# Sorted block attention with a token-mixing MLP: w_out among the casting loads, loads that wait for a batch's V, and a new order

## The chip, the core and the metric

The kernel runs on one core of a Trainium2 chip. The metric is the device time of one execution in microseconds; several executions are timed and the median is given. One execution was taken with the hardware profiler; times "at 33.27" are microseconds from the start of its span. A core has TensorE (PE: matmuls and transposes into PSUM, with its weight loads PEld), VectorE (DVE), ScalarE (ACT), GpSimd (POOL) and SyncE (SP). DMAs are issued by SP or POOL and carried out by 16 DMA engines. A load that changes the type on the way (float32 in memory, bfloat16 in SBUF) is issued by POOL.

## The reference

Four batches, 8 heads, 768 positions of 64, cut into 8 blocks of 96. A matrix P per head (8x8, from `sort_net` by five rounds of softmax-like normalisation) mixes the blocks of K and of V; attention runs inside each block; the result is put through a token-mixing MLP.

```python
P = sort_net
for _ in range(5):
    P = P - np.max(P, axis=-1, keepdims=True)
    P = np.exp(P)
    P = P / (np.sum(P, axis=-1, keepdims=True) + 1e-09)
    P = P / (np.sum(P, axis=-2, keepdims=True) + 1e-09)
k_sorted = einsum('bhij,bhjcd->bhicd', P, k_b);  v_sorted likewise
attn = softmax(q_b @ k_sorted_b.T / 8);  x = attn @ v_sorted_b        # per block
wq, wk = x @ w_q, x @ w_k
W_tok = einsum('bsd,btd->bst', wq, wk) / 8
out = relu(einsum('bst,btd->bsd', W_tok, x)) @ w_out
```

## The kernel before

All work is cut into small items, each one call of a function `u_<letter>`. The string `ORDER` (L18 and on) lists them in the order in which they are issued, and since every engine runs its instructions in that order, the string is the schedule. An item is a letter, a batch, a number and a last sign: for TensorE's items (capitals) the PSUM bank, for the others the engine (A, D, P, S). So `K124` is K of batch 1, part 2, into bank 4, and `k12D` its eviction on VectorE.

The items of a batch, in the order of the data:

- `l` loads: q (`l.0`), k (`l.1`), v (`l.2`) of a batch, 1.5 MB in float32 each, as one casting DMA from POOL (L100) into `Qn`, `Kn` or `Vn`, of which there are three each; `l03` loads `w_q` and `w_k` into `wqk`; `l04` loads `w_out`, in float32, from SP into two of the output buffers `ot`, from which the items `f` cast it into `wo` (one on ACT, two on DVE, one on POOL).
- `c`: the Sinkhorn rounds (ACT for exp, DVE for the rest), ending in `Pb`. `U`, `b`, `B`: TensorE turns it into a mixing matrix, which `n` spreads into `M` (one per batch in two buffers, two halves each; batch 0 on DVE, the others on POOL).
- `Q`/`q`: q transposed to `QT`. `K`/`k`: K mixed and transposed by a matmul with `M`, evicted to `KT`. `V`/`v`: V mixed, evicted to `Vs`. Then `R`: six DMAs from SP a batch that regroup `Vs` into `VT`, one per row `r` of 128 positions; every attention matmul of the batch needs all six.
- `S`/`e`: scores and exp into `E` (seven groups). `P`, `r`, `x`: `E` times `VT` (five groups, `P.4` the small one), one over the row sum, and the product into `X`, both on DVE. `T`/`t`: `X` transposed to `XT`.
- `J`/`j`: the two projections into `qkT`; `d` copies its lower half to the upper partitions of `qD`, by an SP DMA or by an engine. `W`/`w`, `G`/`g`: `wk` and `Ab`. `H`/`h`: relu into `mixT`. `O`/`o`: times `wo`, into `ot`, and `y` stores two rows of output from SP.
- `Z`: so many filler matmuls on zeros (34 in all), which keep TensorE going at the start.

Two batches are in flight at a time. The first loads wait for nothing; a load into a buffer that is used again waits until TensorE has read it. Batch 1's transforms run beside batch 0's attention, and so on.

Of the kernel before, what the change touches and what calls it, by code (L numbers as in the profile page):

```python
# [15 lines left out]


ORDER = """  # L18
l04S l00P l02P l01P i00P i03P i02P l11P l10P l03P l12P l21P l20P l22P c00D Z087 c01D i01D f00P f03D
f02A f01D c02D Z027 c03D Q017 c04D Z026 Q005 q01D Z024 q00A c05D Q027 U006 Z025 q02A b00D Z024 B005  # L20
n01D u00A Z024 n11P n00D Z024 V020 n10P K012 v02A K034 k01D V016 k03A Z021 R04S R05S K002 v01A K020
k00D Z025 k02A V006 R02S l32P l31P l30P R03S Z025 n20P v00A S000 S012 K124 e00A Z027 R01S k12D n21P
R00S K116 e01A S020 Z025 k11D e02A S062 S034 S046 e06A Z021 e03A K132 S050 k13D e04A K104 k10D e05A
Q127 P000 q12D P042 Q106 r00D r04D x00D P034 q10A Q117 x04D P020 q11A r03D P012 r02D x03D S136 e13A
x02D S124 e12A V116 r01D T021 x01D v11A T030 S154 t03D e15A T013 R13S V106 R12S t01D T000 t02A v10D
S144 S162 t00A J011 e16A R11S K226 j01D e14A R10S J000 k22D d01S K212 j00A V124 k21D d00A W007 K230
n31P v12A W016 K202 w01D w00A R14S S104 n30P k20A G007 R15S k23A G017 S112 e10A g01D Q206 e11A H000
H024 q20D Q227 h00A h02D H012 Q216 h01A P130 q21D P104 r13D P122 q22D O026 x13D O047 o02A r10D r12D
x10D S220 O006 e22A o04D S244 o00D P140 e24A O017 x12D P114 o01D V302 r11D T126 y00S r14D v30A x11D
O037 t12A R30S V322 x14D R31S T105 o03D v32A S230 T134 t10D y01S V226 e23A t13D R34S S202 T115 R35S  # L30
v22D J114 e20A K320 t11D j11A R25S K306 k32A R24S K312 d11D k30D W115 J104 k31A w11D S260 S256 j10A
V202 e25A d10D W105 O054 v20D w10A e26A S216 G105 o05A R21S V210 e21A R20S G115 y02S v21D K332 g11A
V316 k33A H124 R23S Q301 v31A h12D R22S Q320 Q313 q30A R32S q32D H106 O152 R33S q31D h10A H110 S354
o15D h11A O143 S306 e35A S360 O112 e36A P244 o14A o11D P200 e30A y12S O133 r24D r20D x24D P346 x20D
o13A O122 S334 r34D o12A P220 x34D O103 e33A y11S r22D x22D P216 o10A S314 r21D P230 y10S e31A x21D
S342 e34A S324 r23D T217 x23D T206 e32A P332 t20D T221 t21A r33D T230 x33D P324 t22A J207 t23D T331
j20A r32D P312 x32D t33A d20S J210 W201 r31D P306 j21A x31D w20A T325 d21S W210 G201 t32A r30D w21D
T314 x30D G211 t31A J310 g21D T307 j31A H222 H204 t30D d31S W316 h22A H210 h20D J307 O253 j30A w31D
h21D d30A W302 O247 o25A w30A O233 o24A G302 y22S o23A O227 G312 o22D O213 g31A y21S H320 H314 o21D
H306 h32A O202 O343 h30A h31D O351 o20A o34D O300 y20S o35A O317 y32S o30D O331 o31A O320 y30S o33D  # L40
o32A y31S
"""


# [1 line left out]
def kernel(  # L46
# [11 lines left out]
    nc = tc.nc  # L58
# [4 lines left out]
    P = 128  # L63
# [21 lines left out]
    def tiles(name, n, shape, dtype=BF16):  # L85
        return [sb.tile(shape, dtype, name=f"{name}{i}") for i in range(n)]
# [10 lines left out]
    wo = sb.tile([P, PT, DM], BF16, name="wo")  # L97

    def load(t, src, b):
        nc.gpsimd.dma_start(out=t[b % NIN].rearrange("p h r d -> p h (r d)"),  # L100
                            in_=src[b].rearrange("h (p r) d -> p h (r d)", p=P))
# [14 lines left out]
    ot = tiles("ot", NOT, [P, 2, DM], FP32)  # L116
# [23 lines left out]
    def copy(e, o, i):  # L140
        if e == "A":
            nc.scalar.copy(o, i)  # L142
        else:
            nc.vector.tensor_copy(o, i)  # L144
# [44 lines left out]
    def u_l(b, n, e):  # L189
        if n == 3:  # L190
            for s, w in enumerate((moe_w_q, moe_w_k)):
                nc.gpsimd.dma_start(out=wqk[:, :, s, :], in_=w.rearrange("(t p) d -> p t d", p=P))
        elif n == 4:
            src = moe_w_out.rearrange("(t p) d -> p t d", p=P)
            for i in range(2):
                nc.sync.dma_start(out=ot[2 + i], in_=src[:, 2 * i:2 * i + 2, :])
        else:
            load((Qn, Kn, Vn)[n], (q, k, v)[n], b)

    def u_f(b, n, e):  # L200
        if e == "P":
            nc.gpsimd.tensor_copy(wo[:, n, :], ot[2 + n // 2][:, n % 2, :])
        else:
            copy(e, wo[:, n, :], ot[2 + n // 2][:, n % 2, :])


    def u_U(b, n, bank):
# [228 lines left out]
    for item in ORDER.split():  # L436
        kind, b, n, arg = item[0], int(item[1]), int(item[2:-1]), item[-1]
# [5 lines left out]
        elif kind in fills:  # L443
            src = (fills[kind], b, 1 if kind == "g" else n)
# [33 lines left out]
```

## Time and profile before

| | us |
|---|---|
| median of 3 runs | 117.53 (116.5 to 118.53) |
| the profiled execution | 116.31 |
| its span, first to last instruction | 114.5 |
| TensorE busy | 94.4 (82%) |
| VectorE busy | 71.2 (62%) |
| ScalarE busy | 70.7 (62%) |
| GpSimd busy | 26.6 (23%) |
| mean granted TensorE clock | 0.937 |

The casting loads (the page calls their queue software_dynamic) took 55.1% of the 16 DMA engines' span, the DMAs issued by SP 27.8%. In the chain that ended last TensorE has 61% of the span and DMAs 21%. A row of the timeline gives start, length, engine, line, operation, the tile written and those read, and in brackets the idle time of the engine ahead of it with what ended it. A row of the groups gives busy time and the mean ns of one, then the idle time ahead. In the windows each engine has its busy time and count, and the last columns are the granted clock, the busy share of the DMA engines (it can pass 1 where an engine has several transfers under way) and GB/s.

### The profile page before, as it was taken

The page shows a single profiled execution, that of the slowest core. Times are in us where ns is not written, and L with a number is a line of the kernel's source. Part 1 is how long each engine was busy: PE and PEld are TensorE (multiplying, and loading weights), DVE is VectorE, ACT ScalarE, POOL GpSimd, SP SyncE. Part 2 cuts the span into 40 slices and gives each one's busy share as a digit, 9 for nine tenths or more (in the row PEclk, how much of TensorE's full clock was granted, in tenths as well). Part 3 has the DMA queues.
Part 4 walks back from the last instruction along what each step waited for, and adds up shares of the span by engine and source line. Part 5 has one row for each costly group of instructions (what it writes and reads, how often), then busy time and mean ns, then how long its engine had stood idle before and what let it go on. Part 6 is the DMA issues. An engine that isn't in the chain of part 4 may idle for free.

```text
span 114.5 us, 3313 instructions
## 1 busy us (share of the span) xinstructions
PE 94.4 (82%) x1408; PEld 61.1 (53%) x1419; DVE 71.2 (62%) x133; ACT 70.7 (62%) x99; POOL 26.6 (23%) x37
## 2 busy tenths in 40 slices
PE   5803956999539799959999999999999999999920
PEld 2202333756338685836746866855569775444400
DVE  2587654435816987335889985592999978236320
ACT  4021351899606599967065989889689757818420
POOL 6999955836900000800000000000000000000000
PEclk9985599999996799996799999999999999999998
DMA  2999999999999999999962880751463100053872
GB/s 36 353 192 203 204 204 204 203 191 243 247 208 203 207 203 214 241 227 230 203 101 82 286 277 15 265 153 50 183 239 133 23 17 17 14 220 137 330 310 94
DMA packets 19646, 20.52 MB, mean 179 GB/s; under 512 B 1968, under 2 KB 17584, under 8 KB 19632
## 3 DMA queue, kind: packets, MB, share of 16 engines
q0 software_dynamic: 13536, 9.57, 55.1%
q1 hardware_dynamic: 6096, 10.74, 27.8%
q8 instruction: 11, 0.18, 0.6%
q14 instruction: 3, 0.02, 0.1%
HBM read 20.19 MB, written 6.29 MB: 231 GB/s over the span
## 4 chain that ended last, share of the span: by engine, by line
PE 61%; DMA 21%; ACT 5%; DVE 5%; issue 4%; SPq 0%; DVEq 0%; ACTq 0%; POOLq 0%
PE ps L138 61%; DMA Qn<-in_q_dram 8%; DMA VT<-Vs 7%; DMA qD<-qkT 6%; ACT E L309 2%; ACT Vs L142 2%; DVE M L226 1%; DVE mixT L416 1%; ACT XT L142 1%; DVE QT L144 1%; ACT ot L142 1%; DVE qkT L144 0%; SPq L279 0%; ACT PTR L142 0%; DVE KT L144 0%
## 5 line engine op out<-in xcount | busy, mean ns | idle before, releaser
L309 ACT ACTIVATE E<-ps 96x960 bf16<-96x960 f32 (+1 forms) x28 | 24.0, 902 | 2.3 <-PE ps L138 2.3
L138 PE MATMUL ps<-wo,mixT 128*128 128x512 bf16 x89 | 22.6, 380 | 0.6 <-issue 0.2
L341 DVE TENSOR_TENSOR X<-ps,R 96x896 bf16<-96x896 f32 (+1 forms) x20 | 19.6, 994 | 0.3
L138 PE MATMUL ps<-VT,E 96*128 96x65 bf16 x256 | 12.1, 206 | 2.9 <-DMA VT<-Vs 2.9
L138 PE MATMUL ps<-idb,Qn 128*64 128x128 bf16 x192 | 9.1, 255 | 5.6 <-DMA Qn<-in_q_dram 5.4
L138 PEld LDWEIGHTS <-E 96*128 96x128 bf16 x256 | 10.7, 106 | 4.7 <-DMA VT<-Vs 3.0
L138 PEld LDWEIGHTS <-mixT 128*128 128x128 bf16 x96 | 8.2, 97 | 9.1 <-issue 1.0
L144 DVE COPY ot<-ps 128x512 f32<-128x512 f32 x11 | 7.6, 688 | 8.6 <-PE ps L138 4.7
L142 ACT COPY ot<-ps 128x512 f32<-128x512 f32 x13 | 7.6, 585 | 7.8 <-PE ps L138 4.3
L144 DVE CAST KT<-ps 128x768 bf16<-128x768 f32 x9 | 8.5, 955 | 5.7 <-PE ps L138 3.9
L138 PE MATMUL ps<-fil 128*128 128x512 bf16 x30 | 11.0, 478 | 1.3 <-DVE fil L153 1.2
L138 PEld LDWEIGHTS <-Qn 128*64 128x64 bf16 x192 | 7.3, 131 | 8.9 <-DMA Qn<-in_q_dram 5.9
L226 POOL TENSOR_TENSOR M<-PTR,m_p 128x512 bf16<-128x512 bf16 x6 | 7.7, 1314 | 14.8 <-PE ps L138 14.8
L142 ACT CAST Vs<-ps 128x1024 bf16<-128x1024 f32 x8 | 8.2, 1030 | 2.9 <-PE ps L138 1.6
L138 PE MATMUL ps<-QT,KT 64*128 64x96 bf16 x256 | 9.6, 208 | 0.2 <-ACT E L309 0.2
L142 ACT COPY QT<-ps 128x1024 bf16<-128x1024 bf16 x5 | 5.1, 1014 | 7.2 <-PE ps L138 7.2
L138 PEld LDWEIGHTS <-KT 64*128 64x128 bf16 x256 | 6.5, 97 | 4.8 <-issue 3.8
L414 ACT ACTIVATE mixT<-ps 128x1024 bf16<-128x1024 f32 x7 | 7.2, 1023 | 3.0 <-PE ps L138 2.9
L138 PE MATMUL ps<-Vn,M 128*128 128x128 bf16 x96 | 7.4, 220 | 1.5 <-DVE M L226 0.9
L416 DVE TENSOR_SCALAR mixT<-ps 128x1024 bf16<-128x1024 f32 x5 | 6.1, 1222 | 3.4 <-PE ps L138 3.3
L138 PE MATMUL ps<-M,Kn 128*64 128x128 bf16 x192 | 7.6, 222 | 0.4
L138 PE MATMUL ps<-idb,X 96*128 96x96 bf16 x128 | 7.6, 207 | 0.0
(68 smaller groups left out, 127.3 us busy)
## 6 DMA issues: line engine op xcount, KB each, us to landing
out_dram<-ot SPq DMA_DIRECT2D x12, 512.0 KB, 2.9
VT<-Vs SPq DMA_DIRECT2D x24, 130.0 KB, 4.7
Qn<-in_q_dram POOLq DMA_DIRECT2D x4, 768.0 KB, 21.1
Vn<-in_v_dram POOLq DMA_DIRECT2D x4, 768.0 KB, 23.8
Kn<-in_k_dram POOLq DMA_DIRECT2D x4, 768.0 KB, 19.4
ot<-in_moe_w_out_dram SPq DMA_DIRECT2D x2, 512.0 KB, 4.0
qD<-qkT SPq DMA_DIRECT2D x4, 48.0 KB, 1.8
wqk<-in_moe_w_q_dram POOLq DMA_DIRECT2D x1, 64.0 KB, 15.6
```

What stands on the lines that cost most here:

```text
L138: nc.tensor.matmul(o, w, x, is_transpose=t, start=start, stop=stop, skip_group_check=True)
L142: nc.scalar.copy(o, i)
L144: nc.vector.tensor_copy(o, i)
L226: ENG[e].tensor_tensor(out=M[b % 2][:, h0:h1], in0=src.unsqueeze(2).to_broadcast([P, 4, SP, NB]), in1=m_p.unsqueeze(1).unsqueeze(3).to_bro ...
L309: nc.scalar.activation(E[b % 2][:, n, 0:2 * w * BLK].rearrange("p (t a c) -> p a t c", a=2, c=BLK), PS[0:BLK, bank:bank + 2, 0:w * BLK].re ...
L341: nc.vector.tensor_mul(xo.rearrange("p (a t d) -> p a t d", a=2, d=D), avps(bank, w)[:, :, :, 0:D], rr[b, n][:, :, 0:w].unsqueeze(3).to_br ...
L414: nc.scalar.activation(o, i, ACT.Relu)
L416: nc.vector.tensor_relu(o, i)
```

## The change

The code changes little: `w_out` is loaded by POOL, casting, straight into `wo`, and the items `f` are gone. `u_N`, which stands in both kernels and was not used before, copies one element of a batch's `Vs` on POOL into a spare cell, so that POOL goes on only when that part of V has been evicted.

```diff
         elif n == 4:
-            src = moe_w_out.rearrange("(t p) d -> p t d", p=P)
-            for i in range(2):
-                nc.sync.dma_start(out=ot[2 + i], in_=src[:, 2 * i:2 * i + 2, :])
+            nc.gpsimd.dma_start(out=wo, in_=moe_w_out.rearrange("(t p) d -> p t d", p=P))
         else:
             load((Qn, Kn, Vn)[n], (q, k, v)[n], b)
-
-    def u_f(b, n, e):
-        if e == "P":
-            nc.gpsimd.tensor_copy(wo[:, n, :], ot[2 + n // 2][:, n % 2, :])
-        else:
-            copy(e, wo[:, n, :], ot[2 + n // 2][:, n % 2, :])
```

The rest is a new `ORDER`. Its first line, before and after:

```diff
-l04S l00P l02P l01P i00P i03P i02P l11P l10P l03P l12P l21P l20P l22P c00D Z087 c01D i01D f00P f03D
+l00P l11P l02P i00P i03P i02P l01P c00D Z087 c01D i01D c02D l03P Z027 c03D Z027 c04D l10P Q026 Q007
```

The loads came in the order w_out, q0 v0 k0, k1 q1 wqk, v1 k2 q2 v2, v3 k3 q3. Now it is q0 k1 v0 k0, wqk q1; then three gates on batch 0's V (`N01v N00v N02v`); v1 q2 k2; three gates on batch 1's V; w_out q3 v2, k3 v3. The 34 fillers are dealt out anew.

GpSimd from its last memset on, before (`Qn_66` to `Qn_68` are the three q buffers, `Kn_69` to `Kn_71` those of k, `Vn_72` to `Vn_74` those of v):

```order
L186 MEMSET E_86 96x608
L100 DMA Kn_70<-in_k_dram 128x8x384
L100 DMA Qn_67<-in_q_dram 128x8x384
L192 DMA wqk<-in_moe_w_q_dram 128x4x64
L192 DMA wqk<-in_moe_w_k_dram 128x4x64
L100 DMA Vn_73<-in_v_dram 128x8x384
L100 DMA Kn_71<-in_k_dram 128x8x384
L100 DMA Qn_68<-in_q_dram 128x8x384
L100 DMA Vn_74<-in_v_dram 128x8x384
L202 CAST wo<-ot_102 128x512
L226 TENSOR_TENSOR M_105<-PTR,m_p 128x512 x2
```

The same engine after, from the load of q1 on (`Vs_81` is batch 0's mixed V, `Vs_82` batch 1's):

```order
L100 DMA Qn_67<-in_q_dram 128x8x384
L218 TENSOR_TENSOR M_105<-PTR,m_p 128x512 x2
L287 COPY gate<-Vs_81 1x1 x3
L100 DMA Vn_73<-in_v_dram 128x8x384
L100 DMA Qn_68<-in_q_dram 128x8x384
L100 DMA Kn_71<-in_k_dram 128x8x384
L218 TENSOR_TENSOR M_104<-PTR,m_p 128x512 x2
L218 TENSOR_TENSOR M_105<-PTR,m_p 128x512
L287 COPY gate<-Vs_82 1x1 x3
L194 DMA wo<-in_moe_w_out_dram 128x4x512
L100 DMA Qn_66<-in_q_dram 128x8x384
L100 DMA Vn_74<-in_v_dram 128x8x384
```

Batch 1's M and both gates now stand among the loads: v1, q2 and k2 follow batch 0's V, and w_out, q3 and v2 (with k3 and v3 behind) follow batch 1's, where all loads but batch 3's three were issued ahead of any M.

SyncE's queue from its start, before (`VT_83` is batch 0's regrouped V, `VT_84` batch 1's):

```order
L92 DMA Pm<-in_sort_net_dram 32x64
L196 DMA ot_102<-in_moe_w_out_dram 128x2x512
L196 DMA ot_103<-in_moe_w_out_dram 128x2x512
L279 DMA VT_83<-Vs_81 16x8x520 x6
L279 DMA VT_84<-Vs_82 16x8x520 x4
L369 DMA qD_93<-qkT_91 64x384
L279 DMA VT_84<-Vs_82 16x8x520 x2
L431 DMA out_dram<-ot_100 128x1024
```

And after:

```order
L92 DMA Pm<-in_sort_net_dram 32x64
L271 DMA VT_83<-Vs_81 16x8x520 x6
L271 DMA VT_84<-Vs_82 16x8x520 x6
L423 DMA out_dram<-ot_100 128x1024
L271 DMA VT_83<-Vs_81 16x8x520 x6
```

The two w_out loads and the copy into `qD` for batch 0 are gone from it; two batches of regroups follow each other directly. Batch 0's `qD` is now filled by VectorE alone, in these rows (before, one half was ScalarE's and one the DMA above):

```order
L144 COPY XT_89<-ps 128x4x192 x3
L144 CAST qkT_91<-ps 128x384
L144 COPY qD_93<-qkT_91 64x384
L144 CAST qkT_91<-ps 128x384
L144 COPY wk_95<-ps 96x256
L144 COPY qD_93<-qkT_91 64x384
L144 COPY wk_95<-ps 96x256
L385 TENSOR_SCALAR Ab_97<-ps 128x256
```

Both copies follow their half of `qkT` at once, ahead of batch 0's `Ab`.

ScalarE around the seven E of batch 0, before (`E_85` batch 0, `E_86` batch 1):

```order
L142 CAST Vs_81<-ps 128x8x2x64
L309 ACTIVATE E_85<-ps 96x2x5x96 x3
L309 ACTIVATE E_85<-ps 96x2x2x96
L309 ACTIVATE E_85<-ps 96x2x5x96 x3
L142 COPY QT_78<-ps 128x4x256 x2
L309 ACTIVATE E_86<-ps 96x2x5x96 x2
L142 CAST Vs_82<-ps 128x8x2x64
```

And after:

```order
L142 CAST Vs_81<-ps 128x8x2x64 x2
L142 CAST KT_80<-ps 128x768 x2
L142 CAST KT_79<-ps 128x768 x2
L301 ACTIVATE E_85<-ps 96x2x2x96
L301 ACTIVATE E_85<-ps 96x2x5x96 x6
L301 ACTIVATE E_86<-ps 96x2x5x96 x3
L142 CAST Vs_82<-ps 128x8x2x64 x3
```

Two evictions of batch 1's K (`KT_80`) now stand ahead of batch 0's K (`KT_79`) and E; batch 1's q copies behind E are VectorE's; three E of batch 1 and all its V evictions, now ScalarE's, follow directly. On TensorE, two Q and three S groups of batch 1 that stood behind the first P of batch 0 stand ahead of it, as do two S groups of batch 2 ahead of the first P of batch 1, and K of batch 1 ahead of K of batch 0.

More of the change, by code (lines that the diff above doesn't have):

```diff
@@ L18 @@
 ORDER = """
-l04S l00P l02P l01P i00P i03P i02P l11P l10P l03P l12P l21P l20P l22P c00D Z087 c01D i01D f00P f03D
[L20 to L38, printed above, removed]
@@ L39 @@
-h21D d30A W302 O247 o25A w30A O233 o24A G302 y22S o23A O227 G312 o22D O213 g31A y21S H320 H314 o21D
-H306 h32A O202 O343 h30A h31D O351 o20A o34D O300 y20S o35A O317 y32S o30D O331 o31A O320 y30S o33D
-o32A y31S
+l00P l11P l02P i00P i03P i02P l01P c00D Z087 c01D i01D c02D l03P Z027 c03D Z027 c04D l10P Q026 Q007
+q02A c05D Z025 q00A Q014 Z025 q01A U007 Z026 b00D B007 n00D u00A Z026 n11P n01D Z026 V010 n10P Z027
+v01A K132 V004 k13D V026 R02S v00A R03S K110 v02D N01v N00v N02v l12P l20P l21P K102 k11A Z025 R01S
@@ new lines @@
+R00S k10A K026 R05S K010 R04S k02D K034 k01A K002 k03D K126 n21P k00A Z021 k12D S062 Z020 e06A n20P
+S004 S040 e00A S032 S026 e03A Z025 S014 e02A S052 e01A Z027 Q126 e05A Q117 q12D Q105 e04A q11D q10D
+S120 S132 S114 e12A P046 r04D e11A P030 x04D e13A r03D V106 x03D P004 v10A V112 r00D V120 x00D v11A
+R11S P016 n30P R10S r01D v12A N10v N11v N12v l04P l30P l22P P024 R13S x01D R12S S142 n31P e14A R15S
+Q201 r02D R14S Q220 x02D q20A Q217 T006 l31P T025 q21A t00D T011 S102 t02A t01D T034 S156 t03D J001
@@ new lines @@
+e10A J015 j00D e15A K202 d00D W001 j01D q22A K216 w00D W015 d01D G001 l32P k21A w01D K224 G011 k20A
+K236 g01D k22A S162 k23D H010 e16A H024 h01D H002 S216 h00A h02D S240 e21A P112 e24A r11D P134 x11D
+P106 O021 r13D r10D x13D S222 O010 o02A e22A x10D S254 Q311 e25A o01D S262 T107 Q326 q31D e26A P124
+t10A q32D S200 P142 r12D e20A O057 x12D O006 o05A r14D x14D T125 o00A V210 t12D T114 y00S v21A V222
+T135 v22D t11A V206 R22S K330 R23S v20A J104 t13D R24S k33D K322 R25S j10A R20S J115 k32A R21S d10D
@@ new lines @@
+W104 K310 j11A w10D K302 k31A d11D W117 G106 k30D S234 O031 e23A w11D V322 o03A V314 v32D y01S G116
+v31A V300 g11D Q307 R35S v30A H102 R32S H114 q30D R34S O046 h10A R33S h11D R30S P220 R31S S322 o04D
+O137 e32A r22D y02S x22D P234 H122 O116 r23D h12A o13D P210 x23D o11A O147 r21D S342 x21D o14A S364
+O156 e36A e34A T217 o15D P240 P204 t21D y12S S312 r24D O126 r20D e31A x24D T227 x20D o12A T231 P312
+y11S t23A t22D S354 T200 r31D e35A S336 x31D J211 t20A P344 j21D P332 e33A r34D J200 d21S x34D W211
@@ L42 @@
+r33D S306 j20A w21D P324 x33D e30A d20S W201 O100 w20A r32D P302 x32D o10A G201 y10S T330 r30D G211
+x30D t33A T327 T316 g21A t32D T300 t31A H222 H214 t30D J311 h22A H206 J300 j31D h21A h20D d31S O251
+j30A W315 d30A W300 O224 w31D o25A w30D G305 o22D O207 G315 o20A O234 g31D H320 O245 o23D y21S H312
+H306 o24D h32A O214 y22S O355 h30D h31A O341 o21A o35A O310 y20S o34D O307 y32S o31A O321 o30A O330
+y30S o32D o33A y31S
 """
```

## The prediction

> **What bounds the kernel now.** I read the slices of the page first, then the chain that ended last, then the timeline of the first 60 us, then the landing times of single loads. The slices:
>
> ```profile
> PE   5803956999539799959999999999999999999920
> PEclk9985599999996799996799999999999999999998
> DMA  2999999999999999999962880751463100053872
> ```
>
> A slice is 2.86 us. From about 54 us on TensorE is full; all its holes lie in the first half, where the DMA row stands at 9. The chain says which holes count (start, length, what):
>
> ```profile
> 1.24 9.29 DMA Qn<-in_q_dram
> ...
> 16.08 0.22 DVE Pb L163
> ...
> 18.98 0.70 DVE M L226
> ...
> 25.57 7.65 DMA VT<-Vs
> ...
> 33.27 5.19 PE ps L138 x106
> ...
> 44.66 6.63 DMA qD<-qkT
> ...
> 103.96 5.57 PE ps L138 x25
> ```
>
> So three DMA waits lead (first Q, batch 0's regroup, the copy into qD), with the Sinkhorn steps between; after that it is TensorE to its last matmul at 109.53, and 5 us of copying and storing behind it, which the change leaves alike. The timeline of those places:
>
> ```profile
> 1.21 0.92 SPq L196 DMA_DIRECT2D ot<-in_moe_w_out_dram  x2
> 2.30 0.88 POOL L100 DMA_DIRECT2D Vn<-in_v_dram  x1
> 2.94 0.26 ACT L157 ACTIVATE Pm<-Pm 32x64 f32<-32x64 f32 x1 [0.92 <-DVE Pm L155]
> 3.17 0.88 POOL L100 DMA_DIRECT2D Kn<-in_k_dram  x1
> 6.19 0.62 ACT L142 CAST wo<-ot 128x512 bf16<-128x512 f32 x1 [2.99 <-DMA ot<-in_moe_w_out_dram]
> 9.62 0.26 ACT L157 ACTIVATE Pm<-Pm 32x64 f32<-32x64 f32 x1 [2.65 <-DVE Pm L163]
> 11.39 0.26 ACT L157 ACTIVATE Pm<-Pm 32x64 f32<-32x64 f32 x1 [1.52 <-DVE Pm L163]
> 17.74 1.04 PE L138 MATMUL ps<-fil 128*128 128x512 bf16 x4
> 21.50 4.67 SPq L279 DMA_DIRECT2D VT<-Vs  x6
> 24.20 0.94 POOL L100 DMA_DIRECT2D Vn<-in_v_dram  x1 [1.59 <-PE ps L138]
> 24.85 5.74 ACT L309 ACTIVATE E<-ps 96x960 bf16<-96x960 f32 x7
> 33.27 0.88 PE L138 MATMUL ps<-VT,E 96*128 96x65 bf16 x22 [2.85 <-DMA VT<-Vs]
> 34.09 0.64 PE L138 MATMUL ps<-idb,Qn 128*64 128x128 bf16 x16
> 35.21 1.07 PE L138 MATMUL ps<-idb,Qn 128*64 128x128 bf16 x16
> 37.86 1.04 PE L138 MATMUL ps<-QT,KT 64*128 64x96 bf16 x20
> 39.57 1.09 DVE L341 TENSOR_TENSOR X<-ps,R 96x896 bf16<-96x896 f32 x1
> 45.96 1.03 ACT L142 CAST Vs<-ps 128x1024 bf16<-128x1024 f32 x1
> 51.32 0.37 PE L138 MATMUL ps<-qD,Ab 64*128 64x512 bf16 x1 [1.42 <-DMA qD<-qkT]
> 54.07 2.18 PE L138 MATMUL ps<-VT,E 96*128 96x65 bf16 x42
> ```
>
> The loads, each asked for alone (KB, us from issue to landing): w_out, then V and K of batch 0 (issued at 2.30 and 3.17), the regroups' least, middle and most, V of batch 3 (issued at 24.20), and two stretches with granted clock, DMA share and GB/s in the last columns:
>
> ```profile
> ot<-in_moe_w_out_dram SPq DMA_DIRECT2D x2, 512.0 KB, 4.0
> Vn<-in_v_dram POOLq DMA_DIRECT2D x1, 768.0 KB, 12.2
> Kn<-in_k_dram POOLq DMA_DIRECT2D x1, 768.0 KB, 15.1
> ...
> DMA to landing us min/median/max: 2.3/4.7/7.7
> ...
> Vn<-in_v_dram POOLq DMA_DIRECT2D x1, 768.0 KB, 27.3
> ...
> 4.00:5.00 1.00, 1.00 (x4) 0.25 (x2) 0.93 (x4) 0.00 (x0) 0.93 (x4) 1.00 1.06 406
> 51.50:56.10 4.60, 4.60 (x82) 3.56 (x79) 2.91 (x5) 2.05 (x2) 0.00 (x0) 0.63 1.28 220
> ```
>
> V lands at 14.5 and K at 18.3: a load takes 3.8 us once the engines are busy with loads, and they come down one by one. Batch 3's V lands at 51.5.
>
> **The change, part by part.** Times below are of the span of the profiled execution, which took 116.31 us with a span of 114.5; the median of the three runs is 117.53, 1.2 above it.
>
> *w_out out of the start.* Its 1 MB lands by 5.2 to 6.2 and Q, issued at 1.24, only at 10.5. Without it Q can land between 6.2 (its issue ends at 2.30, plus 3.8) and 10.5 (if the wait was not w_out's). I take 7.2: 10.5 less 3.3, midway between the 2.6 that w_out's 1.05 MB takes at the 406 GB/s of that stretch and the 4.0 to its landing. By the Trainium skill, page "DMA: Bandwidth & Descriptors", section "Latency and other measured facts", a load issued from GpSimd has its first byte after about 1 us; an estimate by that page is Q at 7.1, so the sum would be the same; no run here shows a first load that starts alone. K of batch 1, V and K of batch 0 follow 3.8 us apart: 11.0, 14.8, 18.6. So K of batch 1 takes w_out's place, and V and K of batch 0 come no earlier than before. The two wqk loads add about 1.3, Q of batch 1 lands near 24 to 26.
>
> *Casts of w_out gone.* ScalarE waited 2.99 for w_out ahead of an exp and cast 0.62; VectorE's casts delayed the next step too. An iteration takes 1.77 (9.62 to 11.39). Five from 2.94, and 0.3 for one reduction between, end at 12.1 and not at 16.3, unless the Q copy that now stands ahead of the last exp is late (it isn't for Q before 8.5). M is then whole at 15.4 (19.7 before). Twelve filler matmuls (0.26 each by the x4 row) follow, so the first V transform starts near 16.5 and not at 19.7.
>
> *What eats that.* From 16.5 TensorE has three V and three K groups of 0.5 to 0.6 (rows below) and 12 fillers more (2.6 to 3.1): it comes to batch 0's K at 21.9 to 22.5, with V and K evictions of about 1 us alternating on two engines beside it. Four K, evicted by two engines (0.96 the slower), end at 24.3. The seven E start at 24.5 against 24.85: nothing is gained here, although M is 4.3 us earlier.
>
> *Regroups.* VT's six DMAs are issued as the V evictions end, at about 18, 21 and 22 (21.5 to 25.6 before). With loads under way one takes 4.7 to 7.7; only one or two loads, not five, are ahead or beside. The last lands at 28 to 30, not at 33.27. The first P needs the sixth E (24.5 plus 6 times 0.9): it starts at 30.4, set by ScalarE. Before it the new order has put two Q and three S groups that stood behind it (0.6, 1.0, and 1.2: 2.8 us). So TensorE is 33.27 + 2.8 - 30.4 = 5.7 us ahead. VectorE's five X (1.09, with R some 1.25 each) end at 37.2 and not at 40.7, 3.5 us ahead, and what follows X is ahead by that; Q of batch 2 fills TensorE in between.
>
> *qD.* For batch 0 both halves are copied on VectorE; the DMA of 6.63 and TensorE's 1.42 go. Batch 1's P then starts when batch 1's regroups have landed and H is through. Batch 1's V lands near 31, its evictions end at 36 to 37, its regroups land near 46; before, P of batch 1 started at 54.07 with two S groups (0.8) yet to come that now stand ahead. P of batch 1 near 46.5 is 8 us ahead (54.07 + 0.8 - 46.5), some of it because the stretch at granted clock 0.63 comes after a wait that is gone.
>
> *The gates.* Six 1x1 copies on GpSimd cost about 0.1 each. Behind the first three wait V of batch 1, Q and K of batch 2 and two M; behind the next three w_out, Q of batch 3, V of batch 2, an M, K and V of batch 3. The first opens near 21.7, while Q of batch 1 is still running, so the queue doesn't run dry; the second at 37, about when K of batch 2 ends. From there: w_out 43 (six regroups are 0.78 MB and move among the loads at some 220 GB/s in all, so they cost the loads about 3), Q of batch 3 47, V of batch 2 51, K of batch 3 55 to 57, and V of batch 3, with the next regroups and the first store beside it, 63 to 64. The old order had it at 51.5 and needed it at 61.
>
> *Who is late next.* The page's groups (busy us of all):
>
> ```profile
> L138 PE MATMUL ps<-VT,E 96*128 96x65 bf16 x256 | 12.1, 206 | 2.9 <-DMA VT<-Vs 2.9
> L144 DVE CAST KT<-ps 128x768 bf16<-128x768 f32 x9 | 8.5, 955 | 5.7 <-PE ps L138 3.9
> L138 PE MATMUL ps<-Vn,M 128*128 128x128 bf16 x96 | 7.4, 220 | 1.5 <-DVE M L226 0.9
> L138 PE MATMUL ps<-M,Kn 128*64 128x128 bf16 x192 | 7.6, 222 | 0.4
> ```
>
> By them a P of 14 is 0.66, a V 0.62, a K of 12 0.48; an O is 0.89 (5.57 for 25 of its matmuls). Between P of batch 1 and V of batch 3 the new order has five P (3.0), five O (4.5), three V and four K (3.8), two Q (1.3) and some 6.4 of other groups of about 0.5: 19 us, of which a group's first 0.1 runs under the one before, 33 times: 16. TensorE is there at 62.5 and waits 1.5 for the load. Behind it remain 55.5 (54.07 to 109.53) less 0.8 less 16: 38.7 us. So 64 + 38.7 = 102.7 against 109.5. (With 19 it is there at 65.5, doesn't wait, and ends at 101.2.)
>
> **Sum.** 6.8 us less: 116.31 - 6.8 = 109.5 in the profiled run's own terms. It was faster than all three runs, the median by 1.2; from the median, 117.53 - 6.8 = 110.7. I give 110.5.
>
> **The rivals.**
>
> *Loads come later than I place them.* If Q lands at 10.5 after all, or regroups and stores take more from the loads, V of batch 3 lands at 67.5 and TensorE ends at 106.2: 3.3 less than before, 113.0, or 114.2 from the median. For it: the DMA engines stand at 1.3 all through the loads, and nothing in this trace shows Q alone. Against it: Q's landing follows w_out's end by one load.
>
> *GpSimd's issue of loads is held up by VectorE.* The rows at 2.30 and 24.20 have 0.88 and 0.94 for issuing a load, early and late, so nothing held those. Were the first load behind each gate held by one VectorE eviction of 0.96, V of batch 3 would land 1.9 later and TensorE end at 104.6: 111.4, or 112.6 from the median. The Trainium skill, page "SBUF — State Buffer", section "SBUF: two separate sides", says that a load issued from GpSimd starves while VectorE runs certain copies, which speaks against moving w_out there; the trace so far doesn't agree.
>
> *No gain, or slower: the second gate.* It hangs on batch 1's last V eviction, and six loads stand behind it. If that eviction came as late as it does now (45.96 + 1.03 = 47.0, not 37), V of batch 3 would land at about 73 and TensorE would end at 111.7, 2.2 us later than now: 118.5, or 119.7 from the median. Not slower up to a landing of 70.8 (109.5 - 38.7); slower by 2% from 73.1 on. Against it: V of batch 1 now runs ahead of four groups that it stood behind.
>
> **How the numbers follow.** Of the median's time: the sum as worked out, 105 to 112: 0.50. Loads later, 112 to 115.1: 0.25. Issue held up: 0.03. The second gate or other new waits taking all of it, within 2%: 0.14; slower by over 2%: 0.08. Two per cent of 117.5, about what a measurement of this kernel can tell from no change, is 2.35 us: faster 0.78, same 0.14, slower 0.08. The likeliest case's own range is 106.5 to 112; for 8 in 10 I reach from 105.5 (loads never waited for, full clock) to 116.5, a little into the case without gain.
>
> **What would show it.** In the new profile: Q's chain piece ends near 7, Pb near 12; the seven E start at 24 to 25; P of batch 0 starts at 30 to 31 with no DMA wait on VT; no DMA wait on qD in batch 0; w_out lands near 43, V of batch 3 near 64, and TensorE's one DMA wait after 55 us, if any, is for that load. I am wrong if TensorE waits for V of batch 1 or 2 for over 2 us, if P of batch 1 starts after 50, or if the queue of loads stands empty at a gate.

## The result, and the profile after

The changed kernel took 109.61 us (median of 4 runs, 108.96 to 111.23) against 117.02 for the kernel before on the same chip: a ratio of 0.936, 95% interval 0.925 to 0.948. Here and below a ratio leaves out executions over 1.5% slower than the quickest of the same kernel, while a median counts all. The profiled execution took 109.1 us with a span of 107.1 (before: 116.31 and 114.5). TensorE's last matmul ends at 102.66, 6.9 us earlier.

The slices of the changed kernel, 2.68 us each:

```profile
PE   5907898996759899969999999999999999999930
PEclk9995589999999999999999999999999999999999
DMA  0999999999999999999999973683451230009784
```

TensorE's holes in the middle are shallower, and the granted clock is full from the seventh slice on: the dips at 6 and 7 that the old row had behind its DMA waits are gone. In windows of a quarter microsecond those dips are two stretches at 0.50, each 3.4 us long (35.2 to 38.6 and 52.3 to 55.7), with TensorE nearly full. My estimate from them is that up to 3.4 of the 6.9 us are the clock's, half of each stretch. The chain that ended last (start, length, what):

```profile
1.25 7.32 DMA Qn<-in_q_dram
...
20.46 0.18 POOL gate L287
...
22.72 18.87 DMA Kn<-in_k_dram
41.59 0.04 issue
41.63 2.92 PE ps L138 x60
...
55.07 8.82 PE ps L138 x137
...
96.87 5.79 PE ps L138 x26
```

Neither a regroup nor `qD` is in it any more. It runs through the first Q, a gate and the load of batch 2's K, and from 41.63 on it is almost all TensorE. The timeline at the places that the prediction named:

```profile
8.62 1.92 PE L138 MATMUL ps<-idb,Qn 128*64 128x128 bf16 x32 [3.18 <-DMA Qn<-in_q_dram]
12.29 0.21 DVE L163 TENSOR_TENSOR Pb<-Pm,tmp 32x64 bf16<-32x64 f32 x1
16.28 0.91 PE L138 MATMUL ps<-Vn,M 128*128 128x128 bf16 x8 [0.44 <-DMA Vn<-in_v_dram]
20.46 0.18 POOL L287 COPY gate<-Vs 1x1 bf16<-1x1 bf16 x1 [0.47 <-DVE Vs L144]
24.12 5.26 ACT L301 ACTIVATE E<-ps 96x960 bf16<-96x960 f32 x6 [0.37 <-PE ps L138]
27.55 1.53 PE L138 MATMUL ps<-idb,Qn 128*64 128x128 bf16 x48 [0.32 <-DMA Qn<-in_q_dram]
28.30 1.89 DVE L144 COPY QT<-ps 128x1024 bf16<-128x1024 bf16 x3 [4.66 <-PE ps L138]
30.24 0.81 PE L138 MATMUL ps<-QT,KT 64*128 64x96 bf16 x30 [1.16 <-DVE QT L144]
30.99 0.43 PE L138 MATMUL ps<-VT,E 96*128 96x65 bf16 x8
33.24 2.87 ACT L142 CAST Vs<-ps 128x1024 bf16<-128x1024 f32 x3
41.63 0.53 PE L138 MATMUL ps<-M,Kn 128*64 128x128 bf16 x12 [0.24 <-DMA Kn<-in_k_dram]
47.50 1.81 PE L138 MATMUL ps<-VT,E 96*128 96x65 bf16 x42
64.38 1.06 PE L138 MATMUL ps<-Vn,M 128*128 128x128 bf16 x16
```

Batch 0's first P starts at 30.99 (33.27 before) with 2.8 us of other groups already done that stood behind it: 5.1 us ahead. Batch 1's starts at 47.50 (54.07 before, and 0.8 more work done): 7.4 ahead. At the end 6.9 are left, so the gain is made before 47.5 and half a microsecond is given back behind it. Batch 1's V is evicted from 33.24 on; the old order finished that at 47.0.

Where time is left, the windows (last three columns: granted clock, DMA share, GB/s) show the first load's start, and the regroups' landings (least, middle, most) are what they were:

```profile
2.50:3.50 1.00, 1.00 (x4) 0.44 (x3) 0.62 (x3) 0.26 (x1) 1.00 (x2) 1.00 0.50 22
3.50:4.50 1.00, 1.00 (x5) 0.34 (x3) 0.86 (x5) 0.00 (x0) 0.93 (x3) 1.00 0.89 88
4.50:5.50 1.00, 0.94 (x5) 0.21 (x3) 0.91 (x5) 0.26 (x1) 1.00 (x2) 1.00 1.26 195
...
DMA to landing us min/median/max: 2.4/5.1/7.6
```

### The profile page after: what moved, and what is told of

The parts are those of the page before. It is cut to its first block, busy times and chain, and to the rows that moved or that the text cites. A ratio compares the mean times of both kernels' runs of the same rounds, so it can differ in the third digit from the quotient of the medians.

```text
span 107.1 us, 3325 instructions
## 1 busy us (share of the span) xinstructions
PE 92.0 (86%) x1406; PEld 59.4 (56%) x1419; DVE 69.4 (65%) x135; ACT 70.9 (66%) x95; POOL 27.3 (26%) x43
## 3 DMA queue, kind: packets, MB, share of 16 engines
q0 software_dynamic: 14064, 10.09, 62.5%
## 4 chain that ended last, share of the span: by engine, by line
PE 61%; DMA 24%; DVE 6%; issue 2%; POOL 2%; ACT 1%; POOLq 0%; ACTq 0%
PE ps L138 61%; DMA Kn<-in_k_dram 18%; DMA Qn<-in_q_dram 7%; DVE mixT L408 2%; DVE M L218 1%; DVE Vs L144 1%; POOL Vn L100 1%; POOL Qn L100 1%; DVE KT L144 1%; ACT ot L142 1%; ACT PTR L142 0%; DVE Ab L385 0%; POOL gate L287 0%; ACTq L142 0%; POOLq L287 0%
## 5 line engine op out<-in xcount | busy, mean ns | idle before, releaser
L142 ACT COPY ot<-ps 128x512 f32<-128x512 f32 x15 | 8.7, 586 | 7.6 <-PE ps L138 7.6
L138 PE MATMUL ps<-VT,E 96*128 96x65 bf16 x256 | 11.1, 194 | 0.6 <-ACT E L301 0.3
L138 PE MATMUL ps<-idb,Qn 128*64 128x128 bf16 x192 | 8.0, 244 | 3.7 <-DMA Qn<-in_q_dram 3.7
L138 PEld LDWEIGHTS <-E 96*128 96x128 bf16 x256 | 9.7, 98 | 2.4 <-issue 0.9
L142 ACT CAST Vs<-ps 128x1024 bf16<-128x1024 f32 x9 | 9.1, 1037 | 2.3 <-PE ps L138 2.2
L138 PEld LDWEIGHTS <-Qn 128*64 128x64 bf16 x192 | 6.7, 125 | 5.7 <-DMA Qn<-in_q_dram 4.6
L144 DVE COPY ot<-ps 128x512 f32<-128x512 f32 x9 | 6.1, 681 | 5.2 <-PE ps L138 5.2
L144 DVE CAST KT<-ps 128x768 bf16<-128x768 f32 x7 | 6.5, 954 | 2.2 <-PE ps L138 2.2
L142 ACT CAST KT<-ps 128x768 bf16<-128x768 f32 x9 | 6.8, 805 | 1.3 <-PE ps L138 1.3
L144 DVE COPY QT<-ps 128x1024 bf16<-128x1024 bf16 x6 | 4.0, 688 | 5.6 <-PE ps L138 5.6
```

The lines of the kernel that those rows point to most:

```text
L138: nc.tensor.matmul(o, w, x, is_transpose=t, start=start, stop=stop, skip_group_check=True)
```

## The experiments

Twelve kernels ran, on four chips. The table has each kernel's median (lowest to highest), that of the kernel before on the same chip, and the ratio where it could be given an interval. The kernel before had medians of 117.02 to 118.67 on the chips, so a difference between rows of different chips is good to 1 or 2 us.

| kernel | us | before there | ratio (95%) |
|---|---|---|---|
| after, no gates | 108.85 (108.69 to 109.48) | 118.42 | 0.929 (0.912 to 0.946) |
| after, w_out at the start | 111.73 (111.27 to 112.27) | 118.42 | 0.952 (0.938 to 0.966) |
| after, half of `qD` by DMA | 115.26 (114.59 to 115.93) | 118.42 | 0.982 (0.967 to 0.997) |
| before, w_out casting, last of the early loads | 115.48 (114.27 to 116.92) | 118.42 | 0.974 (0.945 to 1.002) |
| before, `qD` on VectorE | 119.9 (117.75 to 123.07) | 118.67 | |
| before, both | 117.21 (116.49 to 119.63) | 118.67 | |
| after, `qD` by DMA, the wait filled | 113.76 (113.53 to 114.53) | 118.67 | |
| after, no gates, wqk later | 108.48 (108.3 to 109.16) | 118.67 | |
| before, both, batch 1's third V earlier | 115.39 (112.86 to 115.87) | 118.34 | |
| after, no gates, wqk later, memsets between the first loads | 113.24 (111.25 to 113.61) | 118.34 | |
| the kernel before once more | 119.51 (117.68 to 121.98) | 117.5 | 1.013 (1.005 to 1.020) |
| before, both, V earlier, a wait filled | 111.63 (110.82 to 112.3) | 117.5 | 0.956 (0.949 to 0.962) |

**No gates.** All six gate items are out, and the loads that stood behind the first three follow q1 at once.

```diff
-... l10P Q026 ... v02D N01v N00v N02v l12P l20P l21P K102 ... v12A N10v N11v N12v l04P ...
+... l10P l12P l20P l21P Q026 ... v02D K102 ... v12A l04P ...
```

> The new kernel without its six gates, and with v1, q2, k2 issued right behind q1, as early as before. My theory: the regroups are not helped by the gates (in the new kernel they still take 6.7 to 7.6 us to land) and batch 0's P is held by q of batch 1, so the time stays within 1.5 us of the new kernel's 109.6 and P of batch 0 starts at 31 plus or minus 0.7. Rival, that the gates are what brings the regroups in early: the last regroup of batch 0 lands 3 us later or more, P of batch 0 starts at 33 or later, and the time is 112 or more.

It is as fast as the changed kernel: 0.929 against 0.936, with intervals that overlap almost wholly. Its regroups, now with three more loads in the queue behind the running one:

```profile
DMA to landing us min/median/max: 2.4/4.8/7.8
```

Batch 0's six alone took 6.1, 6.9 and 7.6 us (least, middle, most), and 6.1, 6.8 and 7.6 with the gates. So a regroup does not come sooner because fewer loads are queued; batch 0's first P starts at 31.18 here, as the theory had it. The waits that give the change its name bring nothing that can be measured, and cost nothing either.

**w_out back at the start**, in the new order, loaded by SP in float32 and cast by the four `f` items as before.

```diff
-l00P l11P ... c01D i01D c02D ... v12A N10v N11v N12v l04P l30P ...
+l04S l00P l11P ... c01D i01D f00P f03D f02A f01D c02D ... v12A N10v N11v N12v l30P ...
```

> The new order and its gates, but w_out loaded by SP at the start and cast by the three engines as before. My theory, that w_out's place is worth the larger part: q of batch 0 lands at 10.5, Pb is ready at 15 to 16 instead of 12.5, the loads of batch 0 and 1 come 2 to 3.5 us later and the late loads about level, so the time is 111.5 to 113.5. Rival, that the order alone makes the gain: within 1 us of 109.6. Third, that w_out's place is all of it: 116 or more.

111.73 us, ratio 0.952: some 2 us slower than the changed kernel, and 2.9 slower than the kernel without gates, which ran on the same chip. Its first Q and first V:

```profile
10.45 1.92 PE L138 MATMUL ps<-idb,Qn 128*64 128x128 bf16 x32 [5.14 <-DMA Qn<-in_q_dram]
...
18.23 0.61 PE L138 MATMUL ps<-Vn,M 128*128 128x128 bf16 x8 [0.96 <-DMA Vn<-in_v_dram]
```

Both come 1.8 to 2.0 us later than in the changed kernel (8.62 and 16.28), and the first P of batch 0 is at 32.57, 1.6 later. That is the price of w_out at the start, its casts included.

**Half of `qD` by DMA**, in the new order.

```diff
-... W015 d01D G001 ...
+... W015 d01S G001 ...
```

> The new kernel with one half of batch 0's qD copied by an SP DMA again instead of VectorE. My theory from the prediction's term: TensorE waits 1 to 2 us for qD ahead of H, and the time is 110.3 to 111.5. Rival, that the wait on qD was only a waiting for the regroups in the same queue, which now are through in time: no wait, within 0.7 us of 109.6.

115.26 us: this one copy is worth 0.046 of the old kernel's time, some 5.4 us (6.4 against the kernel without gates on the same chip), where I had put 1.42 and expected 1 to 2. The row of the wait, then four windows behind it:

```profile
48.98 0.58 PE L138 MATMUL ps<-qD,Ab 64*128 64x512 bf16 x1 [3.67 <-DMA qD<-qkT]
```

```profile
45.00:49.00 4.00, 0.33 (x3) 0.04 (x5) 0.80 (x1) 0.45 (x2) 0.00 (x0) 0.77 1.32 207
49.00:52.00 3.00, 2.88 (x37) 2.25 (x37) 2.36 (x2) 1.55 (x2) 0.00 (x0) 0.50 1.32 204
52.00:55.00 3.00, 3.00 (x40) 2.23 (x38) 2.39 (x5) 1.18 (x2) 0.00 (x0) 0.50 1.32 204
55.00:58.00 3.00, 3.00 (x26) 1.04 (x24) 1.37 (x3) 1.48 (x2) 0.00 (x0) 0.60 1.32 204
```

The DMA was issued at 42.42 and landed 6.5 us later. TensorE stands 3.67, and then works at a granted clock of 0.50 until about 57.4 (in the last window, 0.60 is 2.4 us at 0.50 and 0.6 at 1.00). The clock had fallen within the stand already, at 47.2.

**The same wait, filled.** Seventeen filler matmuls stand ahead of the matmul that waits for `qD`; nothing else differs from the last kernel.

```diff
-... k23D H010 ...
+... k23D Z0170 H010 ...
```

> The kernel of the run with qD by DMA, with 17 filler matmuls (3.6 us at full clock) placed ahead of H of batch 0, where TensorE otherwise stands 3.7 us. My theory: the 5.6 us that the DMA cost are the 3.7 of standing and some 2 of the granted clock of 0.50 that follows for 8 us; with the fillers the clock stays near 1.00 and the time is 112.5 to 113.8. Rival, that the clock has other reasons: 115 or more, clock again near 0.5 behind H.

113.76 us, 1.5 less although TensorE does 17 matmuls more, but on another chip. The same stretch:

```profile
45.00:49.00 4.00, 3.84 (x26) 1.70 (x21) 1.18 (x2) 0.84 (x2) 0.00 (x0) 1.00 1.31 208
49.00:52.00 3.00, 2.16 (x47) 1.57 (x47) 2.51 (x3) 2.12 (x3) 0.00 (x0) 1.00 1.31 203
```

The two profiles tell more than the medians. Batch 0's first P starts at 31.25 and 31.29, so they are level up to there; the last matmul ends at 108.98 and 106.28. So the lower clock costs 2.7 us in these executions (the first is the slowest of its kernel's four) and 1.5 by the medians, and the standing itself some 3.7: with the fillers TensorE still ends 3.6 later than in the changed kernel (102.66).

**The code's two parts in the old order.** First `w_out` alone, casting, last of the early loads:

```diff
-l04S l00P l02P l01P ... l21P l20P l22P c00D Z087 c01D i01D f00P f03D f02A f01D c02D ...
+l00P l02P l01P ... l21P l20P l22P l04P c00D Z087 c01D i01D c02D ...
```

> The kernel before with one thing changed: w_out loaded by POOL, casting, as the load behind v2, and its casts gone. My theory: q of batch 0 lands at 7 to 8.6, Pb at about 12.5, batch 0's P 3 to 4 us earlier than 33.27, and the wait on qD stays; time 112.5 to 114.5. Rival, that the order makes the gain: 115.5 to 117.5, since the old order's fillers, regroups and waits stay. Third, that w_out's place is all of it: 110 or less.

115.48 us, 0.974 with an interval that reaches 1.002: a gain of up to some 6 us or none. Its first Q comes at 8.69, not 10.5, and its first P at 31.56, but it still waits 3.03 there for the last regroup. Then `qD` alone, and both together:

```diff
-... k22D d01S K212 ...
+... k22D d01D K212 ...
```

> The kernel before with only the qD copy of batch 0 that SP issued moved to VectorE. My theory: in the old order TensorE stands for it 1.4 us, and behind it stands the landing of batch 1's last regroup at 53.9, so P of batch 1 starts no earlier than 53 and the time falls by 0 to 1.5 us, to 115.5 to 117. Rival, that this DMA is the main cost in the old order too (as its 5.6 us in the new one): P of batch 1 starts near 50 and the time is 112 or less.

> The kernel before, old order, with both parts that can be taken over alone: w_out as a casting load behind v2, and batch 0's qD by VectorE. My theory: the rest of the gain is in the order, above all in the q, S and V groups moved ahead of batch 0's P and in the V evictions of batch 1 that come 10 us earlier; the time is 113 to 115.5. Rival, that these two are the whole gain and the new order adds nothing: 109.5 to 111.

`qD` alone shows no gain (its two quickest runs 117.75 and 118.28, against 115.69 and 117.34 of the kernel before). Both together took 117.21, which is no clear gain either and misses the 113 to 115.5 that I expected. The row and the windows of both together:

```profile
55.51 1.51 PE L137 MATMUL ps<-VT,E 96*128 96x65 bf16 x42 [2.15 <-DMA VT<-Vs]
```

```profile
30.00:34.00 4.00, 2.46 (x42) 2.23 (x43) 1.30 (x3) 0.06 (x1) 1.17 (x1) 0.58 1.32 204
34.00:38.00 4.00, 4.00 (x71) 3.51 (x71) 2.24 (x6) 1.98 (x3) 0.00 (x0) 0.50 1.32 205
38.00:42.00 4.00, 3.52 (x48) 3.12 (x48) 2.68 (x4) 2.99 (x4) 0.00 (x0) 0.50 1.31 203
42.00:46.00 4.00, 4.00 (x56) 3.17 (x54) 2.35 (x4) 3.41 (x5) 0.00 (x0) 0.72 1.25 216
```

Without the wait for `qD` another stands in its place: batch 1's last regroup, whose V the old order evicts late. And the wait of 2.99 for batch 0's regroup is followed by 12 us at a granted clock of about 0.50, in which TensorE is nearly full, so what the earlier start gave is lost there. With w_out alone the first P starts at the same time (31.56, and 31.54 here), but its profile has only 3.4 us of low clock behind it: batch 1's last V is evicted from 44.42 on, here from 47.62, and batch 1's P starts at 52.56 without a wait for a regroup. So how long the clock stays low decides as well which wait is the next, and these runs do not settle what `qD` would be worth in the old order at full clock.

**Both, and batch 1's third V earlier.** The old order with both parts; the V and its eviction go up, its regroups behind the first regroup of the batch.

```diff
-... t02A v10D S144 ... R10S J000 ... j00A V124 k21D ... n31P v12A W016 ... R14S S104 ... R15S k23A ...
+... t02A v10D V124 v12A S144 ... R10S R14S R15S J000 ... j00A k21D ... n31P W016 ... S104 ... k23A ...
```

> The old order with both code parts (the output weight cast late, the diagonal blocks made on VectorE), and the third V projection of batch 1 with its eviction moved up right behind the diagonal blocks, its regroups behind the first regroup of that batch. Theory (what stands behind the diagonal blocks' wait in the old order is the last regroup of batch 1, 2.15 us waited for at 55.5): the regroup lands 4 to 5 us earlier, P of batch 1 starts at 51.5 to 52.5 and the time is 113.5 to 115. Rival (the regroup isn't the bound there, or the V eviction moved up delays batch 0's own chain by as much): within 1 us of the 117.2 that the same kernel took without the move.

115.39 us, between the two expectations. P of batch 1 starts at 53.95 with no wait for a regroup, later than the 51.5 to 52.5 that I expected; the granted clock was 0.50 from 29.9 to 43.6 in this profile, and from 30.6 to 44.3 in the last. The profiled execution took 114.93 us and the quickest 112.86. So the regroup was the wait there, but not all that held the old order.

**A wait in the old order, filled.** Two kernels were meant to have twelve fillers ahead of batch 0's first P: the kernel before, and the one just described.

```diff
-... e05A Q127 P000 ...
+... e05A Q127 Z0122 P000 ...
```

> The kernel before with one edit: twelve filler matmuls (some 3 us) ahead of batch 0's first P, in the 2.85 us in which TensorE stands for the last regroup. Theory (standing there costs the kernel before more than the 2.85 us, through the granted clock behind it, which was 0.86 and 0.67 in the 7 us after the wait): the granted clock stays at 1.00 from 33 to 44, the time is 1 to 3 us under the kernel before on the same chip, and its runs spread less than those of the kernel before (5.0 us from lowest to highest in the last twelve). Rival (TensorE isn't the bound there, VectorE's X is): the clock rises and the time stays within 1 us, with the same spread.

> The old order with both code parts and the third V of batch 1 moved up, and the same twelve fillers ahead of batch 0's first P. Theory (the old order's remaining handicap is the granted clock of 0.50 from 31 to 43): clock 1.00 there, P of batch 1 at 50 to 51.5 instead of 53.95, the time 110.5 to 113. Rival (the order behind it holds the time, not the clock): within 1.5 us of the 115.4 without fillers.

In the first the edit was missing from the order that ran, so that it is the kernel before itself and tells nothing of fillers. As a control it tells something else: against itself the kernel before came out at 1.013 (1.005 to 1.020), so a ratio within some 2% of 1 means nothing for it. In two profiles of this one program the stretch behind the same wait (2.85 and 2.76 us, ending at 33.27 and 34.11) differs; the kernel before as first profiled:

```profile
33.00:36.00 3.00, 2.73 (x68) 2.53 (x68) 2.00 (x5) 1.01 (x1) 0.00 (x0) 0.87 1.32 204
36.00:40.00 4.00, 3.40 (x64) 2.95 (x61) 2.88 (x6) 2.52 (x3) 0.00 (x0) 0.67 1.32 204
```

And once more:

```profile
33.00:36.00 3.00, 1.89 (x34) 1.80 (x36) 0.70 (x3) 0.00 (x0) 0.00 (x0) 0.60 1.31 205
36.00:40.00 4.00, 4.00 (x70) 3.48 (x68) 2.24 (x5) 2.02 (x2) 0.00 (x0) 0.50 1.32 207
```

The spans were 114.5 and 116.5. At 0.50 the clock stood from 35.2 to 38.6 in the first, and from 33.6, within the wait, to 40.4 in the second. The second kernel had the fillers: 111.63 us, 0.956 (0.949 to 0.962). The same stretch, and its two first P:

```profile
33.00:36.00 3.00, 2.83 (x80) 2.43 (x75) 2.67 (x5) 2.05 (x3) 0.00 (x0) 1.00 1.31 203
36.00:40.00 4.00, 3.40 (x74) 3.17 (x74) 3.82 (x7) 4.00 (x5) 0.00 (x0) 1.00 1.32 205
```

```profile
31.88 0.87 PE L137 MATMUL ps<-VT,E 96*128 96x65 bf16 x22 [0.18 <-DMA VT<-Vs]
...
50.71 1.51 PE L137 MATMUL ps<-VT,E 96*128 96x65 bf16 x42 [0.38 <-DMA VT<-Vs]
```

The first P starts no earlier, yet batch 1's is at 50.71 and not at 53.95, though the latter is from one of that kernel's slower executions. The two kernels ran on different chips, so I put the fillers' worth at 1 to 4 us (111.63 against 112.86, the other's lowest run, and 115.39, its median); 1.2 is the part that the quick executions bear out. By ratios, the old order with these four edits has 4.4% of the 6.4%; which parts of the new order make the other 2% was not tested.

**Room beyond the changed kernel.** Without gates, wqk is loaded behind q1 and two more loads:

```diff
-... c02D l03P Z027 ... l10P l12P l20P l21P Q026 ...
+... c02D Z027 ... l10P l12P l20P l03P l21P Q026 ...
```

> The new kernel without gates (108.85), and with wqk loaded behind q2 instead of ahead of q1. My theory: q1, which TensorE waits for ahead of batch 0's P, lands 1.2 us earlier, P of batch 0 starts at 30 instead of 31.2, q2 lands at 35.2, and k2 (41.5) is what TensorE then waits for, 0.5 to 1.5 us: 108.0 to 108.7. Rival, that k2's landing bounds all of it: no difference, 108.6 to 109.2.

108.48 us, the lowest median of all; its first P is at 30.80 (31.18 without the move). Against the kernel with no gates it is 0.4 less, on another chip, which settles nothing between these two. Then two memset items of GpSimd go between its first load and its second, to see whether writing the next loads slows the first:

```diff
-l00P l11P l02P i00P i03P i02P ...
+l00P i00P i03P l11P l02P i02P ...
```

> The kernel without waits between the loads and with the QK weights loaded after the first three, and GpSimd's two memsets moved between the first load and the second. Theory (writing the descriptors of the next loads slows the first one): the first Q projection starts at 7.2 to 7.6 instead of 8.6, later landings come up to 1 us earlier, and the time is 107.5 to 108.0. Rival (the slow start is the first load's own): the first Q projection stays at 8.4 to 8.8, the later loads come 0 to 1 us later, and the time is 108.3 to 109.2.

113.24 us: worse than both expected. The first Q still starts at 8.52, and the windows of the first load read alike:

```profile
8.52 1.65 PE L137 MATMUL ps<-idb,Qn 128*64 128x128 bf16 x32 [2.46 <-DMA Qn<-in_q_dram]
...
18.40 0.61 PE L137 MATMUL ps<-Vn,M 128*128 128x128 bf16 x8 [3.72 <-DMA Vn<-in_v_dram]
```

```profile
2.50:3.50 1.00, 1.00 (x4) 0.44 (x3) 0.61 (x4) 0.26 (x1) 0.94 (x2) 1.00 0.48 18
3.50:4.50 1.00, 1.00 (x4) 0.30 (x2) 0.86 (x5) 0.00 (x0) 0.93 (x2) 1.00 0.91 95
4.50:5.50 1.00, 1.00 (x4) 0.34 (x3) 1.00 (x2) 0.11 (x1) 1.00 (x2) 1.00 1.29 197
```

So the slow start isn't made by GpSimd's writing of the next loads. But those, issued 3 us later, land 2 us later: batch 0's V is waited for 3.72, the first P is at 34.06 (30.80 without), and the time is longer by some 3 us in its two quickest runs (111.25 and 111.52), 4.8 by the median. So a load that landed 2 us later cost about 3. Behind the 3.72 the clock was 0.50 for 3.4 us, which is part of it.

## Why the prediction was right, and where its steps were not

The time was forecast at 110.5 (105.5 to 116.5) and came to 109.61; TensorE's last matmul was put at 102.7 and ended at 102.66. That closeness is part luck, as the steps show.

- *w_out out of the start.* Right in kind, too large in size: 3.3 was put, and it is some 2 us by its experiment. Q did not land at 7.2 but at 8.57: "10.5 less 3.3" took no account of the load's slow start (22, 88, then 195 GB/s), which may have run beside w_out before. By the Trainium skill's page "DMA: Bandwidth & Descriptors", section "Latency and other measured facts", I had an estimate of 7.1; the trace has 8.57, and what the estimate lacked is the slow rate behind the first byte. The next loads came some 1.5 us later than placed (V at 16.28 for 14.8), and q1 at 27.55, where 24 to 26 stood.
- *Sinkhorn and M.* Forecast 12.1 and 16.5 for `Pb` and the first V transform; measured 12.5 and 16.28. Right in the numbers, and for `Pb` in the mechanism. But M was whole at 16.7, not 15.4, and the first V transform began with the half of M that was there, right behind its load (0.44 in the row), not behind a whole M and the fillers. That 16.28 came so near 16.5 is luck.
- *What eats that.* The first, small E starts at 23.26 and the other six from 24.12 (24.5); they end at 29.4, against 30.6 before. So 1.2 us were gained, where "nothing is gained here" stood.
- *Regroups and the first P.* At 30.99 for 30.4, but not "set by ScalarE": near in number, by another wait. The E were through at 29.4; TensorE came to batch 1's Q when q1 landed (27.55), its copies began on VectorE at 28.30, and the scores that stand ahead of P waited for them to 30.24. Those Q and S groups of batch 1, which I counted only as work brought forward, are what P waits for. That "only one or two loads, not five," would help the regroups was not so either.
- *qD.* The mechanism was right and the term mis-sized: "TensorE's 1.42 go" was the old order's price. In the new one the same DMA costs 5.4 us, since P of batch 1 no longer has anything else to wait for, since TensorE comes to it 2.9 us after its issue (5.2 before), and since the clock falls in the wait. In the old order no gain was seen; in the profile of both parts the next wait stood right behind it, after a long stretch of low clock.
- *P of batch 1* at 47.50 for 46.5, by the forecast's route: V's evictions at 33.2 to 36.1 (ending at 36 to 37), no wait for regroups, and H just through: the 0.74 us that TensorE stood before it ended with `mixT`.
- *The gates.* Forecast to cost 0.1 each and to open at 21.7 and 37; they took 0.18 each, opened at 20.6 and 36.4, and the queue did not run dry. Right, but their whole benefit was nil, which only the experiment shows. The rival that saw the second gate eat the gain never came near.
- *Who is late next.* The sum had TensorE wait 1.5 us for batch 3's V to land at 64. The load came at 61.1 and TensorE at 64.16 (its weight load; the matmul at 64.38), 16.7 us behind P of batch 1 as worked out (16 to 19). So the wait that I added was not there, and TensorE was later than "62.5" by about as much: two errors of some 1.5 us that cancelled. The loads ahead of it were misplaced both ways: batch 2's K landed at 41.6, not 37, and w_out at 45.6, not 43, but from there to batch 3's V it took 15.5 us, not 21. TensorE's waits for loads behind batch 0's first P were two, for batch 2's Q (0.22) and K (0.24).
- *Issue held up.* GpSimd took 0.82 to 1.02 us for each load (0.77 for the two of wqk), beside busy VectorE too. The starving that the Trainium skill's page "SBUF — State Buffer", section "SBUF: two separate sides", describes is not seen here. But beside these issues VectorE read PSUM or worked on pieces of 32x64, with one copy from SBUF to SBUF of 0.25 us (into `qD`, at 41.37), so the copies that the page names were hardly put to the test.

What the forecast lacked altogether is the granted clock as a price of standing. It noted 0.63 behind a wait in the old profile (1.42 us, for `qD`), and never put a number on it.

## What to carry to other kernels

Several waits in a row on one path hide each other: price each against the order in which it will stand, and expect an edit that removes one to show its worth only with the next ones gone (`qD`: no gain seen in the old order, 5.4 us in the new). Where TensorE stands on the path that bounds the kernel, try idle matmuls in the wait or move work into it, since the clock behind it comes on top: 1.5 to 2.7 us behind a stand of 3.67. A short stand is not safe by these runs, nor is a long one always punished. A headline part of a change (here the gates) deserves its own experiment before it is copied: what made this change fast was w_out off the start, `qD` on an engine, and the order, which evicts batch 1's V early and leaves no long stand behind the first Q.

## What the runs showed of the hardware

- Behind many stands of TensorE the granted clock fell to 0.50 and stayed there though TensorE was full again. Added up from windows of a quarter microsecond, every such stretch in the fourteen profiles lasts 3.4, 6.8, 10.2 or 13.65 us: one, two, three or four times 3.41. It was 10.2 around a stand of 3.67 (`qD` by DMA; 8.4 of it behind), 13.65 around 2.99 (old order, both parts; 12.7 behind), 3.4 behind 3.72 (memsets moved; 19.1 to 22.5), and 6.8 around the first Q's 3.18 in the changed kernel. The Trainium skill, page "TensorE: Matmul & The Clock Gate", section "Part 1: The HAM clock gate", has the full clock back after about 3.4 us of sustained work; the shortest stretches here agree, the others are two to four times as long.
- The length of the stand does not tell how long, or whether. Behind 1.42 and 1.33 us (the kernel before, twice, ahead of `qD`) the clock was low for 3.4 each time; behind 2.15 (old order, both parts) and 1.54 (w_out casting) it did not fall; 3.03 had 3.4 behind it (w_out casting) and 2.42 had 13.65 around it (batch 1's V earlier). The waits of 1.16 and 0.74 in the changed kernel did nothing.
- The low stretch differs between executions of one program too (3.4 and 6.8 us around the same wait of the kernel before). The old kernel's runs spread by 4.0 to 5.8 us on the four chips, those of the changed kernel by 2.3, without gates by 0.8. That the low stretches make the spread is my reading, not shown; `qD` by DMA has the long wait and spreads by 1.3.
- In the changed kernel a regroup of 130 KB took 6.0 to 7.6 us from issue to landing beside loads (batches 0 and 1), however many were queued, and 2.4 to 4.3 for batches 2 and 3, issued from 58.5 on, with the last load landing at 61.1.
- The first casting load took 7.3 us for 768 KB (written), where the following ones came 3.8 apart: some 200 GB/s are reached only about 3.5 us after its issue, with GpSimd writing the next loads meanwhile (195) or its memsets (197).
